# Blocks of 512 tokens in two of three passes over a feed-forward layer, one accumulation carried across the passes, and the next layer taken from the far end

## The chip, the cores and the metric

The kernel runs on one core of one Trainium2 chip. The metric is the device time of one execution in microseconds (us); less is better. TensorE (PE) multiplies, VectorE (DVE) and ScalarE (ACT) work on elements, GpSimd (POOL) and SyncE (SP) mostly issue DMAs. Every instruction queue runs in order.

## The reference

Three layers over 2304 tokens (4 sequences of 576) with 512 channels: retention in 8 heads of 64, a feed-forward layer of 2048 hidden channels, and a gated one of 1536.

```python
scores = scale * np.matmul(q, k.transpose(0, 1, 3, 2))
ret = np.matmul(scores * Dmat[None], v)            # Dmat: decay by head, lower triangle
x = ret.transpose(0, 2, 1, 3).reshape(B * S, H * D)

h = x @ w_in                                       # layer 1: 512 -> 2048 -> 512
g = np.where(h >= 1, h, np.where(h <= -1, 0.0, (h + 1) ** 2 / 4))
x = g @ w_out

out = ((x @ w_a) * (x @ w_b)) @ w_out2             # layer 2: 512 -> 1536 -> 512
```

## The kernel before, in words

All products are made from float32 values split into a high and a low part, so that one product of 128x128 weights is three matmuls (high by high, high by low, low by high). Activations lie with channels in the partitions and tokens in the columns; a matmul takes a block of TB = 384 tokens, and there are NB1 = 6 blocks. All of them pass through `mm` (L156), so every PE row of the profile has line L157; the name of the tile tells the stage.

**Layer 1** is done in three passes over the 16 chunks of 128 hidden channels (GROUPS1, L26): pass 1 takes the first 3, 4 or 6 chunks of a block, pass 2 goes on to chunk 10, pass 3 takes chunks 11 to 15. A step is one chunk f of one block: `l1` (L648) makes `ph` by 12 matmuls from x and w_in; `act1_parts` (L658) runs ACT twice (L661, L662), DVE (L664), and splits the result into the two halves of a tile `g` on ACT (L669) and DVE (L671); `l2` (L688) adds 12 matmuls from g and w_out into the block's four `acc` banks. `l2` of a step is issued after `l1` of the next, so that 24 matmuls (`l2` of the step before, `l1` of the step after) lie between a `ph` and the use of its `g`. Between passes a block's four banks are emptied to DRAM: `y_out` (L709) copies or adds them, `fetch_y` (L704) brings the partial sums back before the next pass' end. The x of each block is written to DRAM in pass 1 (`xd`) and fetched again for each block of pass 2 and 3 (`fetch_x`, L644), at the second step of the block ahead (L1206). Finished blocks go to DRAM as `yf`.

**Layer 2** works in three super-blocks of 768 tokens. `load_y` (L723) reads a super-block into the tile `b`, on POOL's queue. `right` (L743) forms sums of its four quarters with DVE (the first is L757) and splits them on ACT (L739) and DVE (L740) into seven right factors `tx`. A `Quad` (L797) makes one 2x2 block of a product from seven products of 6 matmuls each in banks qx, qy and qz; `keep` (L788, ACT L793) copies a bank to a tile of the pool t2, so that the bank can go on, and DVE combines them (L815, L822, L828). The seventh product goes on in the bank of c22, so PE has to wait for that copy. `act2` (L844) multiplies the two halves of the gate, of which the first (L848) is c11 of both quads, and splits them for the second product (L840, L841).

Pass 1 is in an order written out by hand. From pass 2 on the order of each engine is set by a scheduler that simulates the program; weights are converted in between, from raw tiles that POOL's queue fetches (L184), as credits allow (PACE, L1164).

For super-block 0, `b` is asked for at the start of block 3 of pass 3 (L1198), and the factors are made during block 5, the last. Pools: t2 has 8 buffers of 384 columns (partial sums, kept banks), g has 3, tx and b are opened before pass 2.

Of the kernel before, what the change touches and what calls it, by code (L numbers as in the profile page):

```python
# [36 lines left out]
CHUNKS = 4  # L37
SPARE, INTER_FIRST = (4, 5), 6
# [81 lines left out]
def retention_ffn_kernel(  # L120
# [21 lines left out]
    gpool = ctx.enter_context(tc.tile_pool(name="g", bufs=3))  # L142
# [89 lines left out]
    for f in range(GROUPS1[-1][-1][1]):  # L232
# [3 lines left out]
        for i, blocks in enumerate(GROUPS1) for b, fs in enumerate(blocks) for f in range(*fs)  # L236
# [400 lines left out]
    def x_space(name):  # L637
        return [dpool.tile([P, 2, NCC, TB], F32, name=f"{name}{b}") for b in range(NB)]

    xd = x_space("xd")  # L640
    yd = [[dpool.tile([P, NCC, TB], F32, name=f"y{i}_{b}") for b in range(NB)] for i in range(2)]
    yf = [dpool.tile([P, NCC, TB], F32, name=f"yf{b}") for b in range(NB)]

    def fetch_x(b, space):  # L644
        t = xpool.tile([P, 2, NCC, TB], F32R, tag="x", name="x")
        nc.sync.dma_start(t.bitcast(F32), space[b])
        return t


    def l1(x, w):  # L650
# [8 lines left out]
    def act1_parts(ph):  # L659
        t = tpool.tile([P, TB], F32, tag="t", name="t")  # L660
        nc.scalar.activation(t, ph[:, :TB], AF.Relu, bias=0.5, scale=0.5)  # L661
        nc.scalar.activation(t, t, AF.Square)  # L662
        yield
        nc.vector.scalar_tensor_tensor(  # L664
            out=t, in0=t, scalar=1.0, in1=ph[:, :TB], op0=ALU.min, op1=ALU.max
        )
        yield
        g = gpool.tile([P, 2, TB], F32R, tag="g", name="g")
        hi = nc.scalar.copy(g[:, 0, :], t)  # L669
        yield g  # L670
        anchor[:] = [hi, nc.vector.tensor_sub(g[:, 1, :], t, g[:, 0, :].bitcast(F32))]  # L671
        yield

    def act1(ph, between=lambda: None):
        parts = act1_parts(ph)
# [12 lines left out]
    def l2(step, out=True):  # L688
        i, b, f, first, last = step
        if first:  # L690
            ys[i, b] = accs(NCC)
        y, w, g = ys[i, b], weights["o", f], gs.pop(step)
# [9 lines left out]
    yin = {}  # L702

    def fetch_y(i, b):  # L704
        for m in range(NCC):
            t = yin[b, m] = t2pool.tile([P, TB], F32, tag="t2", name="yin")
            nc.sync.dma_start(t, yd[i - 1][b][:, m, :])

    def y_out(i, b):  # L709
        for m, y in enumerate(ys.pop((i, b))):  # L710
            if i == 0:
                own, tag = (t2pool, "t2") if stage else (y1pool, "yst")
                t = own.tile([P, TB], F32, tag=tag, name="yst")
                (nc.scalar.copy if m % 2 or not stage else nc.vector.tensor_copy)(t, y[:, :TB])
            else:
                t = yin.pop((b, m))
                nc.vector.tensor_add(t, y[:, :TB], t)
            (nc.gpsimd if stage is None else nc.sync).dma_start((yd[i] if i < 2 else yf)[b][:, m, :], t)
# [3 lines left out]
    factors, uses, given = {}, {}, {}  # L722

    def load_y(n):

        if n >= NSB:
            return
        t = given[n] = bpool.tile([P, NCC, 2 * HT], F32, tag="b", name="b")
        t0 = 2 * HT * n
        while t0 < 2 * HT * (n + 1):  # L730
            b, o = divmod(t0, TB)
            m = min(TB - o, 2 * HT * (n + 1) - t0)
            at = t0 - 2 * HT * n
            nc.gpsimd.dma_start(t[:, :, at:at + m], yf[b][:, :, o:o + m])
            t0 += m
# [6 lines left out]
    def right(n):  # L742


        if n >= NSB:
            return
        sub = nc.vector.tensor_sub
        b = given.pop(n)
        b11, b12 = b[:, 0:2, 0:HT], b[:, 0:2, HT:]
        b21, b22 = b[:, 2:4, 0:HT], b[:, 2:4, HT:]  # L750
        t = bpool.tile([P, 2, HT], F32, tag="tt", name="tt")
# [36 lines left out]
    def keep(o, own=False):  # L788

        t = (tpool if own else t2pool).tile(  # L790
            [P, TB], F32, tag="t" if own else "t2", name="keep"
        )[:, :HT]
        kept_by[0] = nc.scalar.copy(t, o[:, :HT])  # L793
        return t
# [43 lines left out]
    def split_g(t):  # L838
        g = gpool.tile([P, 2, TB], F32R, tag="g", name="g2")
        nc.scalar.copy(g[:, 0, :HT], t)  # L840
        nc.vector.tensor_sub(g[:, 1, :HT], t, g[:, 0, :HT].bitcast(F32))  # L841
        return g

    def act2(qa, qb):  # L844
# [7 lines left out]
        for j, (ca, cb) in enumerate(((qa.c12, qb.c12), (qa.c22, qb.c22))):  # L852
            t = late[f + j] = (
                ca if f + 2 == NF2 else ypool[0].tile([P, HT], F32, tag="y", name="gl")
# [77 lines left out]
    def second_layer(n, quad, other):  # L932


        t0, t1 = 2 * HT * n, 2 * HT * n + HT
# [47 lines left out]
    def l2_2(ys, f, g):  # L983
        w = weights[f]
        for m in (0, 2, 3, 1):
            ws = slice(m * P, (m + 1) * P)
            for i, (a, z) in enumerate(((0, 0), (1, 0), (0, 1))):
                mm(
                    ys[m][:, :HT], w[:, a, ws], g[:, z, :HT],
# [39 lines left out]
    def end_tile(keep=0):  # L1029
# [15 lines left out]
    steps = [  # L1045
        (i, b, f, f == f0, f == f1 - 1)
        for i, blocks in enumerate(GROUPS1) for b, (f0, f1) in enumerate(blocks)
        for f in range(f0, f1)
    ]

    def needed(step):
# [20 lines left out]
        "E": lambda b: nc.gpsimd.dma_start(xd[b], xt[b].bitcast(F32)),  # L1072
    }

    def first_product(k):
        i, b, f, *_ = steps[k]
        ph, ops = l1(xt[b], weights["i", f])
        for o in ops:
            mm(*o)
        gen[k] = act1_parts(ph)  # L1080
# [20 lines left out]
    for s, step in enumerate(steps[:last_by_hand]):  # L1101
# [13 lines left out]
        ph, ops = l1(x, weights["i", f])  # L1115
# [8 lines left out]
        gs[step] = act1(ph, between)  # L1124
# [10 lines left out]
        if first:  # L1135
            nc.gpsimd.dma_start(xd[b], x.bitcast(F32))
# [10 lines left out]
    stage = first_sb.enter_context(tc.tile_pool(name="stage", bufs=1))  # L1147

# [5 lines left out]
    for s, step in enumerate(steps):  # L1154
# [4 lines left out]
        if (i, b, first) == (1, NB - 3, True):  # L1159
            raws2.held = True  # L1160
        if (i, b) == (1, NB - 3) and f >= f1 - 3:
            raws1.fetch_to(2 * GROUPS1[1][0][1] + f - f1 + 4)
        if (i, b, first) == (2, NB - 2, True):
            depth[0], raw_every[0], raw_pools[1:] = 2, 5, []  # L1164
        credit += 1.0 if i == 0 else PACE
# [5 lines left out]
        while credit >= 1.0:  # L1171
            with behind():
                make_more(2 * GROUPS1[1][0][1] if i == 0 or (i == 1 and b < NB - 2) else len(stream))
            credit -= 1.0
        if first:
            if i == 0:
                x = xt[b]
            else:
                x = xt.pop((i, b)) if (i, b) in xt else fetch_x(b, xd)
        ph, ops = l1(x, weights["i", f])  # L1180
# [4 lines left out]
        gs[step] = act1(ph)  # L1185
# [3 lines left out]
        if i == 0 and first:  # L1189
            nc.sync.dma_start(xd[b], x.bitcast(F32))  # L1190
        if i > 0 and first:
            fetch_y(i, b)
        if i == 2 and b == 3 and first:
            load_y(0)
        if i == 2 and b == NB - 1 and first:
            making = right(0)
        if i == 2 and b == NB - 1:
            for _ in range(1 + (not first)):  # L1198
                make_right()
        if f == f0 + 1:  # L1200
            ni, nb = (i, b + 1) if b + 1 < NB else (i + 1, 0)
            if 0 < ni < 3:
                xt[ni, nb] = fetch_x(nb, xd)
        if i == 2 and b == NB - 1:
            load_to(9)

    rx.close()
    ypool[0] = first_sb.enter_context(tc.tile_pool(name="y", bufs=NF2 - 2))
# [10 lines left out]
    for n in range(NSB):  # L1219
# [61 lines left out]
        for j, (acc_of, f, _) in enumerate(todo):  # L1281
# [7 lines left out]
            if j == NF2 - 1:  # L1289
                o_out(ys2, 2 * HT * n + HT)  # L1290
        o_out(early, 2 * HT * n)
# [26 lines left out]
```

## Time and profile before

| | |
|---|---|
| median of 3 runs | 875.59 us (874.38 to 876.51) |
| the profiled execution | 874.88 us, of which the span of its instructions is 873.0 us |
| granted clock of TensorE over the span | 0.998 |
| PE busy | 862.5 us (99%) |
| PE weight loads busy (they overlap PE) | 847.7 us (97%) |
| DVE, ACT, POOL busy | 577.4 us (66%), 446.5 us (51%), 81.1 us (9%) |
| DMA | 238.31 MB, mean 273 GB/s |

How to read it: the profile is of one execution. Pass 1 and the retention end at about 190 us of the span, passes 2 and 3 run to 476 us, layer 2 from there to 873 us. The durations of matmuls are those of a pipeline: the next one starts before the last one's time is over, so the price of a matmul is the distance between two starts. "Released by" is the event that ended an idle time.

### The profile page before, as it was taken

The numbers are of one execution on the slowest core, as the hardware profiler recorded it, in microseconds if no ns is written. First come the engines' busy times: TensorE is split into PE (matmuls) and PEld (weight loads), VectorE is DVE, ScalarE is ACT, GpSimd is POOL, SyncE is SP. The second block draws the span as 40 slices with busy tenths as digits, with TensorE's granted clock in tenths as the row PEclk, the third lists the DMA queues.
The fourth block names the chain that finished last, engine by engine and source line by source line (L and its number), as shares of the span: only waits on it lengthen the run. The fifth ranks groups of instructions, "written<-read, shape, count | busy, mean of one in ns | idle before, by whom it ended". The sixth has DMA issues, their size and how long they took to land.

```text
span 873.0 us, 16378 instructions
## 1 busy us (share of the span) xinstructions
PE 862.5 (99%) x6308; PEld 847.7 (97%) x6308; DVE 577.4 (66%) x1088; ACT 446.5 (51%) x899; POOL 81.1 (9%) x124
## 2 busy tenths in 40 slices
PE   8899999999999999999999999999999999999998
PEld 6799999999999999999999999999999999999998
DVE  5787556576777789777779858752347575246465
ACT  4556355575766677666567546442233353333253
POOL 2313233110010011011001000000000000000000
PEclk9999999999999999999999999999999999999999
DMA  9997581648679889899889998879547589847583
GB/s 337 356 337 255 204 279 58 263 149 315 241 258 329 309 291 322 329 352 331 286 302 323 404 410 263 257 245 338 174 145 245 187 276 413 324 146 245 185 288 151
DMA packets 81373, 238.31 MB, mean 273 GB/s; under 512 B 8424, under 2 KB 35304, under 8 KB 78992
## 3 DMA queue, kind: packets, MB, share of 16 engines
q1 hardware_dynamic: 71616, 196.87, 63.2%
q0 software_dynamic: 9664, 40.37, 13.4%
q8 instruction: 50, 0.82, 0.4%
q14 instruction: 27, 0.22, 0.1%
q10 hardware_dynamic: 16, 0.02, 0.0%
HBM read 175.89 MB, written 61.34 MB: 272 GB/s over the span
## 4 chain that ended last, share of the span: by engine, by line
PE 99%; issue 1%; DVE 0%; ACT 0%
PE acc L157 35%; PE ph L157 23%; PE qx L157 17%; PE qy L157 9%; PE late L157 4%; PE qz L157 4%; PE po L157 4%; PE s L157 2%; PE idle L157 1%; PE wacc L157 0%; DVE keep L849 0%; DVE warm L1001 0%; ACT ost L976 0%
## 5 line engine op out<-in xcount | busy, mean ns | idle before, releaser
L157 PE MATMUL acc<-g,w 128*128 128x384 f32 x1296 | 249.0, 334 | 0.0
L157 PEld LDWEIGHTS acc<-g,w 128*128 128x128 f32 x1296 | 226.5, 188 | 0.4
L157 PE MATMUL ph<-x,w 128*128 128x384 f32 x1152 | 220.9, 336 | 0.0
L157 PEld LDWEIGHTS ph<-x,w 128*128 128x128 f32 x1152 | 201.6, 188 | 0.8 <-issue 0.2
L157 PE MATMUL qx<-tx,w 128*128 128x384 f32 x864 | 164.7, 334 | 0.0
L157 PEld LDWEIGHTS qx<-tx,w 128*128 128x128 f32 x864 | 151.1, 188 | 0.0
L793 ACT COPY keep<-qx 128x384 f32<-128x384 f32 x126 | 59.6, 480 | 141.3 <-PE qx L157 133.5
L661 ACT ACTIVATE t<-ph 128x384 f32<-128x384 f32 x96 | 47.1, 490 | 79.3 <-PE ph L157 75.1
L664 DVE SCALAR_TENSOR_TENSOR t<-t,ph 128x384 f32<-128x384 f32 x96 | 52.8, 551 | 51.9 <-ACT t L662 51.5
L157 PE MATMUL qy<-tx,w 128*128 128x384 f32 x432 | 86.3, 334 | 0.0
L157 PE MATMUL acc<-sp,w 128*128 128x384 f32 x432 | 77.5, 334 | 0.0
L157 PEld LDWEIGHTS qy<-tx,w 128*128 128x128 f32 x432 | 75.9, 188 | 0.0
L157 PEld LDWEIGHTS acc<-sp,w 128*128 128x128 f32 x432 | 75.1, 188 | 0.0
L669 ACT CAST g<-t 128x384 fp32r<-128x384 f32 x96 | 49.0, 510 | 40.7 <-DVE t L664 34.8
L671 DVE TENSOR_TENSOR g<-t,g 128x384 fp32r<-128x384 f32 x96 | 53.5, 557 | 20.8 <-ACT g L669 20.5
L886 DVE TENSOR_TENSOR sp<-gb,sp 128x768 fp32r<-128x768 f32 x42 | 40.1, 956 | 21.3 <-ACT sp L885 21.0
L662 ACT ACTIVATE t<-t 128x384 f32<-128x384 f32 x96 | 50.5, 526 | 2.7
L885 ACT CAST sp<-gb 128x768 fp32r<-128x768 f32 x42 | 35.1, 837 | 32.3 <-PE acc L157 18.8
L196 ACT ACTIVATE raw<-raw 128x512 int32<-128x512 uint32 x68 | 45.6, 671 | 2.7 <-DMA raw<-in_moe_w_out 2.7
L828 DVE TENSOR_TENSOR keep<-keep 128x384 f32<-128x384 f32 x36 | 20.0, 557 | 40.4 <-ACT keep L793 40.4
L157 PE MATMUL qz<-tx,w 128*128 128x384 f32 x216 | 43.4, 334 | 0.0
L815 DVE TENSOR_TENSOR keep<-qz,keep 128x384 f32<-128x384 f32 x36 | 20.0, 556 | 32.1 <-PE qz L157 27.7
(113 smaller groups left out, 944.9 us busy)
## 6 DMA issues: line engine op xcount, KB each, us to landing
w<-q SPq DMA_DIRECT2D x126, 512.0 KB, 5.3
q<-q SPq DMA_DIRECT2D x42, 512.0 KB, 7.1
w<-o SPq DMA_DIRECT2D x42, 512.0 KB, 5.1
x<-xd SPq DMA_DIRECT2D x12, 1536.0 KB, 8.6
u<-in_qkv SPq DMA_DIRECT2D x32, 512.0 KB, 8.3
raw<-in_moe_w_out POOLq DMA_DIRECT2D x18, 512.0 KB, 6.5
yin<-y SPq DMA_DIRECT2D x48, 192.0 KB, 4.3
xd<-x POOLq DMA_DIRECT2D x5, 1536.0 KB, 8.7
```

Of the source, the lines that this page charges most:

```text
L157: return nc.tensor.matmul(o, l, r, start=start, stop=stop, skip_group_check=goes_on)
L196: nc.scalar.activation(r, low, AF.Copy, scale=2.0 ** -29)
L661: nc.scalar.activation(t, ph[:, :TB], AF.Relu, bias=0.5, scale=0.5)
L662: nc.scalar.activation(t, t, AF.Square)
L664: nc.vector.scalar_tensor_tensor(out=t, in0=t, scalar=1.0, in1=ph[:, :TB], op0=ALU.min, op1=ALU.max)
L669: hi = nc.scalar.copy(g[:, 0, :], t)
L671: anchor[:] = [hi, nc.vector.tensor_sub(g[:, 1, :], t, g[:, 0, :].bitcast(F32))]
L793: kept_by[0] = nc.scalar.copy(t, o[:, :HT])
L815: anchor[:] = [kept_by[0], nc.vector.tensor_add(self.c11, z[:, :HT], self.c11)]
L828: nc.vector.tensor_add(self.c22, self.c22, self.s5)
L885: nc.scalar.copy(t[:, 0], b)
L886: nc.vector.tensor_sub(t[:, 1], b, t[:, 0].bitcast(F32))
```

## The change

From token 768 on, passes 2 and 3 work in blocks of 512 tokens: blocks 0 and 1 of 384, then three of 512 (NWIDE = 5). Pass 1 keeps its six blocks, so x and the partial sums of tokens 768 to 2303 lie in one DRAM tile each, whose slices both sizes address. The blocks of pass 3 come in the order 4, 3, 2, 0, 1. Block 4, the last of pass 2, is the first of pass 3 and goes on in its four banks: it isn't emptied and fetched in between. The x tiles of blocks 4 and 3 stay in two pools (xw0, xw1) from pass 2 to pass 3. Super-blocks run from the last tokens to the first. The tiles t, g become 512 wide, g's halves are tiles of their own; t2 has 7 buffers in place of 8, and `gl` of the first chunk takes a buffer of the conversion pool. The pools of the factors are opened on the other side of memory, before the last two blocks of pass 3, where `b` is now asked for too (second-last block).

```diff
+WIDE = 512
+NWIDE = 2 + 3 * (NB1 - 2) // 4
 GROUPS1 = [
     [(0, 3), (0, 4)] + [(0, 6)] * (NB1 - 2),
-    [(3, 11), (4, 11)] + [(6, 11)] * (NB1 - 2),
-    [(11, 16)] * NB1,
+    [(3, 11), (4, 11)] + [(6, 11)] * (NWIDE - 2),
+    [(11, 16)] * NWIDE,
 ]
+PASSES = [range(NB1), range(NWIDE), [4, 3, 2, 0, 1]]
...
-    gpool = ctx.enter_context(tc.tile_pool(name="g", bufs=3))
+    gpool = ctx.enter_context(tc.tile_pool(name="g", bufs=6))
...
+    def width(i, b):
+        return WIDE if i and b > 1 else TB
...
+    xd = in_parts("xd", (2, NCC))
+    y0 = in_parts("y0", (NCC,))
...
-                ops.append((ph[:, :TB], w[:, a, ws], x[:, z, cc, :]))
+                ops.append((ph[:, :n], w[:, a, ws], x[:, z, cc, :]))
...
-                mm(y[m][:, :TB], w[:, a, ws], g[:, z, :], first and n == 0, last and n == 2)
+                mm(y[m][:, :k], w[:, a, ws], g[z], first and n == 0, last and n == 2)
...
+    def first_token(n):
+        return 2 * HT * (NSB - 1 - n)
...
+                ca if f + 2 == NF2
+                else ypool[0].tile([P, HT], F32, tag="y", name="gl") if f
+                else cpool.tile([P, 512], F32, tag="conv", name="gl")[:, :HT]
...
+                (i, b, f, f == f0 and (i, b) != (2, goes_on), f == f1 - 1 and (i, b) != (1, goes_on))
...
-    t2pool = ctx.enter_context(tc.tile_pool(name="t2", bufs=8))
-    txpool = ctx.enter_context(tc.tile_pool(name="tx", bufs=5))
-    bpool = ctx.enter_context(tc.tile_pool(name="b", bufs=1))
+    t2pool = ctx.enter_context(tc.tile_pool(name="t2", bufs=7))
...
+    wide[:] = [
+        ground.enter_context(tc.tile_pool(name=f"xw{n}", bufs=1, side="right")) for n in range(2)
+    ]
+    ywide[0] = ground.enter_context(tc.tile_pool(name="yw", bufs=YBUFS, side="right"))
...
+        if (i, b, begins) == (2, PASSES[2][-2], True):
+            ground.close()
+            rx.close()
+            txpool[0] = ctx.enter_context(tc.tile_pool(name="tx", bufs=5, side="right"))
+            bpool[0] = ctx.enter_context(tc.tile_pool(name="b", bufs=1, side="right"))
-        credit += 1.0 if i == 0 else PACE
+        credit += 1.0 if i == 0 else PACE * width(i, b) / TB
...
-        if i == 2 and b == 3 and first:
+        if i == 2 and b == PASSES[2][-2] and begins:
             load_y(0)
...
-            if 0 < ni < 3:
-                xt[ni, nb] = fetch_x(nb, xd)
+            if (ni, nb) in ((2, goes_on), (2, goes_on - 1)):
+                xt[ni, nb] = xt[1, nb]
+            else:
+                xt[ni, nb] = fetch_x(ni, nb)
...
-    ypool[0] = first_sb.enter_context(tc.tile_pool(name="y", bufs=NF2 - 2))
+    ypool[0] = first_sb.enter_context(tc.tile_pool(name="y", bufs=NF2 - 4))
```

How the scheduler's order moves, at the three places that the prediction speaks of. In brackets stand the semaphores that an instruction waits for: DMAHW and DMASW are DMAs, the others engines; PE, without waits, shows its order alone.

**SP, at the end of pass 1.** First before, where the spill of the last x, the fetch of x for block 0 of pass 2 and the first partial sums follow each other:

```order
L1190 DMA xd5_180<-x_2153 128x3072 [waits DMAHW5_49,DVE_49]
L646 DMA x_2606<-xd0_175 128x3072 [waits DMASW5_49,DMASW2_49,DMAHW6_49,DMASW0_49,PE_49]
L718 DMA y0_4_185<-yst_2544 128x384 [waits DMAHW7_49,Activation_49]
L718 DMA y0_4_185<-yst_2541 128x384 [waits DMAHW0_49,DVE_49]
L718 DMA y0_4_185<-yst_2550 128x384 [waits DMAHW1_49,Activation_49]
L718 DMA y0_4_185<-yst_2547 128x384 [waits DMAHW2_49,DVE_49]
L646 DMA x_2882<-xd1_176 128x3072 [waits DMAHW3_49,DMASW7_49,DMAHW5_49,DMASW1_49,PE_49]
```

and now, where the xw are 512 wide and xdw and y0w are the DRAM tiles of tokens from 768 on:

```order
L740 DMA yin_3546<-y0w_180 128x512 [waits DMASW6_49,DMASW4_49]
L1248 DMA xdw_177<-x_2164 1024x1x384 [waits DVE_49]
L672 DMA xw_3602<-xdw_177 128x8x512 [waits DMAHW2_49,DMASW7_49,DMASW5_49]
L672 DMA x_2628<-xd0_175 128x3072 [waits DMAHW3_49,PE_49]
L672 DMA xw_3269<-xdw_177 128x8x512 [waits DMAHW4_49,DVE_49]
L753 DMA y0w_180<-yst_2565 128x384 [waits DMAHW5_49,Activation_49]
L753 DMA y0w_180<-yst_2562 128x384 [waits DMAHW6_49,DVE_49]
L753 DMA y0w_180<-yst_2571 128x384 [waits DMAHW7_49,Activation_49]
L753 DMA y0w_180<-yst_2568 128x384 [waits DMAHW0_49,DVE_49]
```

The fetch of x for block 0 now stands behind four partial sums of block 2 and the first wide x (2048 KB), and another wide x stands behind it.

**ACT and DVE, at the start of super-block 0.** ACT before; keep_5919 and keep_5835 are c11 of the two quads, keep_5927 is c22 of the first:

```order
L793 COPY keep_5919<-qx_5912 128x384 [waits DMAHW6_49,DMAHW5_49,PE_49]
L220 CAST w_5728<-stage_5722 128x512 [waits DVE_49]
L793 COPY keep_5880<-qx_5828 128x384 [waits PE_49]
L196 ACTIVATE raw_5779<-raw_5779 128x512 [waits DMASW7_49,Activation_49]
L220 CAST w_5776<-stage_5722 128x512 [waits DVE_49]
L382 CAST qo_5896<-stage_5722 128x256 [waits DVE_49]
L793 COPY keep_5927<-qx_5828 128x384 [waits DMAHW7_49,PE_49]
```

ACT now; keep_5537 and keep_5621 are c11 of the two quads, keep_5629 is c22 of the first:

```order
L832 COPY keep_5663<-qx_5614 128x384 [waits PE_49]
L386 CAST qo_5598<-stage_5423 128x256 [waits DVE_49]
L386 CAST qo_5672<-stage_5423 128x256 [waits DMAHW1_49,DMAHW4_49,DVE_49,PE_49]
L386 CAST qo_5672<-stage_5423 128x256
L832 COPY keep_5629<-qx_5530 128x384 [waits DVE_49]
L880 CAST g2_5739<-keep_5537 128x384
```

DVE now, where keep_5621 is completed, read for the last time, and then c22 is worked on:

```order
L380 TENSOR_TENSOR stage_5423<-stage_5423 128x256 [waits DVE_49]
L387 TENSOR_TENSOR qo_5598<-stage_5423,qo_5598 128x256 [waits Activation_49]
L854 TENSOR_TENSOR keep_5621<-qz_5641,keep_5621 128x384 [waits DMAHW2_49,PE_49]
L888 TENSOR_TENSOR keep_5537<-keep_5621,keep_5537 128x384 [waits DVE_49]
L387 TENSOR_TENSOR qo_5672<-stage_5423,qo_5672 128x256 [waits DMAHW4_49,DMAHW1_49,Activation_49]
L387 TENSOR_TENSOR qo_5672<-stage_5423,qo_5672 128x256 [waits Activation_49]
L867 TENSOR_TENSOR keep_5629<-keep_5629,keep_5546 128x384 [waits Activation_49]
```

PE now, around it; tx_5516 goes on in the bank that keep_5629 copies:

```order
L161 MATMUL qx_5530<-tx_5470,w2_5307 128x384 x6
L161 MATMUL qx_5614<-tx_5470,w2_5417 128x384 x6
L161 MATMUL qz_5641<-tx_5411,w2_5365 128x384 x6
L161 MATMUL qx_5696<-tx2_5299,w2_5419 128x384 x6
L161 MATMUL qx_5530<-tx_5516,w2_5309 128x384 x6
L161 MATMUL acc0_5522<-g2_5739,w_4820 128x384 x2
```

The copy of c22 waited for PE and a DMA before and waits for DVE now: its tile of pool t2 is that of keep_5621, which L888 (L848 before) reads last.

**POOL, in the last blocks of pass 3.** Before, the first piece of `b` (384 tokens) is asked for two raw tiles ahead of the second:

```order
L184 DMA raw_4919<-in_moe2_w_a 128x4x128 [waits DMASW7_49,DVE_49,Activation_49]
L734 DMA b_5146<-yf0_193 128x4x384 [waits DMAHW4_49,DMAHW2_49,DMAHW5_49,DMAHW1_49,DMAHW6_49,DMAHW0_49,PE_49]
L184 DMA raw_4964<-in_moe2_w_a 128x4x128 [waits DMASW2_49,DVE_49]
L184 DMA raw_5096<-in_moe2_w_b 128x4x128 [waits DMASW1_49,DVE_49,Activation_49]
L734 DMA b_5146<-yf1_194 128x4x384 [waits DMAHW2_49,DMAHW7_49,DMAHW1_49,DMAHW0_49]
L184 DMA raw_5157<-in_moe2_w_b 128x4x128 [waits DMASW3_49,DVE_49,Activation_49]
```

and now:

```order
L188 DMA raw_5006<-in_moe2_w_b 128x4x128 [waits DMASW1_49,DVE_49,Activation_49]
L188 DMA raw_5013<-in_moe2_w_b 128x4x128 [waits DMASW4_49,DVE_49,Activation_49]
L188 DMA raw_5203<-in_moe2_w_out 128x512 [waits DMASW6_49,DVE_49,Activation_49]
L772 DMA b_5064<-yf3_189 128x4x256 [waits DMAHW3_49,DMAHW4_49,DMAHW2_49,DMAHW5_49,DMAHW1_49,DMAHW6_49,DMAHW0_49,DMAHW7_49,DMASW3_49,DVE_49]
L772 DMA b_5064<-yf4_190 128x4x512
L188 DMA raw_5243<-in_moe2_w_out 128x512 [waits DMASW5_49,DMASW0_49,DVE_49]
```

Both pieces (256 and 512 tokens) are asked for together, behind three raw tiles that wait for ACT and DVE.

## Rows read from the trace of the kernel before

**Rows 1.** The page: busy time, and the chain that ended last.

```profile
PE 862.5 (99%) x6308; PEld 847.7 (97%) x6308; DVE 577.4 (66%) x1088; ACT 446.5 (51%) x899; POOL 81.1 (9%) x124
...
PE 99%; issue 1%; DVE 0%; ACT 0%
```

**Rows 2.** Windows: PE, PEld, DVE, ACT, POOL busy us; clock, DMA share, GB/s.

```profile
190.00:362.00 172.00, 172.00 (x994) 172.00 (x994) 134.66 (x281) 114.56 (x243) 19.56 (x28) 1.00 0.82 288
362.00:476.00 114.00, 114.00 (x660) 114.00 (x659) 90.40 (x189) 72.72 (x157) 8.89 (x13) 1.00 0.90 321
```

**Rows 3.** The chain, one of its pieces: start, us, what, number of instructions.

```profile
702.76 23.23 PE acc L157 x134
```

**Rows 4.** PE's timeline, 512-wide matmuls: start, us, what.

```profile
12.60 0.50 PE L157 MATMUL idle<-warm 128*128 128x512 f32 x1
...
12.93 0.39 PE L157 MATMUL idle<-warm 128*128 128x512 f32 x1
...
13.16 0.40 PE L157 MATMUL idle<-warm 128*128 128x512 f32 x1
```

**Rows 5.** PE's timeline, 384-wide matmuls behind a wait.

```profile
582.72 0.44 PE L157 MATMUL late<-g,w 128*128 128x384 f32 x1 [0.65 <-DVE keep L849]
...
583.00 0.34 PE L157 MATMUL late<-g,w 128*128 128x384 f32 x1
...
583.17 0.34 PE L157 MATMUL late<-g,w 128*128 128x384 f32 x1
```

**Rows 6.** Groups by form, 190 to 476 us: busy, mean ns, idle before.

```profile
L157 PE MATMUL acc<-g,w 128*128 128x384 f32 x814 | 156.8, 334 | 0.0
...
L664 DVE SCALAR_TENSOR_TENSOR t<-t,ph 128x384 f32<-128x384 f32 x67 | 36.8, 551 | 29.7 <-ACT t L662 29.3
...
L205 DVE SCALAR_TENSOR_TENSOR stage<-raw,stage 128x512 uint32<-128x512 uint32 x27 | 18.6, 689 | 0.5
```

**Rows 7.** Timeline at the start of super-block 0, PE, DVE and ACT.

```profile
478.41 1.20 PE L157 MATMUL qz<-tx,w 128*128 128x384 f32 x6
...
480.46 0.55 DVE L815 TENSOR_TENSOR keep<-qz,keep 128x384 f32<-128x384 f32 x1
481.05 0.56 DVE L848 TENSOR_TENSOR keep<-keep 128x384 f32<-128x384 f32 x1
...
481.70 0.48 ACT L793 COPY keep<-qx 128x384 f32<-128x384 f32 x1 [0.70 <-DVE keep L848]
```

**Rows 8.** Timeline at 581 us: PE, then DVE released by it.

```profile
580.86 1.20 PE L157 MATMUL qx<-tx,w 128*128 128x384 f32 x6
...
582.10 0.56 DVE L849 TENSOR_TENSOR keep<-qx,keep 128x384 f32<-128x384 f32 x1 [0.25 <-PE qx L157]
```

**Rows 9.** POOL's timeline, the last spill of x on it, and PE then.

```profile
151.49 0.54 POOL L1136 DMA_DIRECT2D xd<-x  x1
...
152.01 0.09 POOL L559 MEMSET turn<- 1x1 f32 x1
...
152.65 0.46 PE L157 MATMUL po<-ret,u 64*64 64x64 f32 x16
```

**Rows 10.** Fetch of x for pass 2: issue, first use, landing.

```profile
169.73 0.33 SPq L646 DMA_DIRECT2D x<-xd  x1
...
194.50 0.68 PE L157 MATMUL ph<-x,w 128*128 128x384 f32 x3
...
x<-xd SPq DMA_DIRECT2D x12, 1536.0 KB, 8.6
```

**Rows 11.** Fetch of b: last block's start, first use, POOL's wait, landing.

```profile
446.17 0.51 PE L157 MATMUL ph<-x,w 128*128 128x384 f32 x2
...
453.23 0.95 DVE L757 TENSOR_TENSOR tt<-b 128x768 f32<-128x768 f32 x1
...
471.17 0.53 POOL L184 DMA_DIRECT2D raw<-in_moe_w_out  x1 [27.51 <-ACT keep L793]
...
b<-yf POOLq DMA_DIRECT2D x6, 768.0 KB, 9.0
```

More of the change, by code (lines that the diff above doesn't have):

```diff
@@ L37 @@
 CHUNKS = 4
+YBUFS = 5
 SPARE, INTER_FIRST = (4, 5), 6
@@ L235, in retention_ffn_kernel @@
         f: (i, b)
-        for i, blocks in enumerate(GROUPS1) for b, fs in enumerate(blocks) for f in range(*fs)
+        for i, blocks in enumerate(GROUPS1) for b in PASSES[i] for f in range(*blocks[b])
     }
@@ L634, in rounds_to, with first_of, in_parts, part @@
             output_next()
[L637 to L646, printed above, removed]
+    def width(i, b):
+        return WIDE if i and b > 1 else TB
+    def first_of(b):
+        return TB * b if b < 2 else 2 * TB + WIDE * (b - 2)
+    def in_parts(name, shape):
+        two = [dpool.tile([P, *shape, TB], F32, name=f"{name}{b}") for b in range(2)]
+        rest = dpool.tile([P, *shape, NB * TB - 2 * TB], F32, name=f"{name}w")
+        def part(i, b):
+            n = width(i, b)
+            return two[b] if b < 2 else rest[(slice(None),) * (1 + len(shape)) + (
+                slice(n * (b - 2), n * (b - 1)),)]
+        return part
+    xd = in_parts("xd", (2, NCC))
+    y0 = in_parts("y0", (NCC,))
+    y1, yf = (
+        [dpool.tile([P, NCC, width(1, b)], F32, name=f"{name}{b}") for b in range(NWIDE)]
+        for name in ("y1", "yf")
+    )
+    wide, ywide, ground = [None, None], [None], ExitStack()
+    def fetch_x(i, b):
+        if b < 2:
+            t = xpool.tile([P, 2, NCC, TB], F32R, tag="x", name="x")
+        else:
+            t = wide[b % 2].tile([P, 2, NCC, WIDE], F32R, tag="xw", name="xw")
+        nc.sync.dma_start(t.bitcast(F32), xd(i, b))
         return t
-    def l1(x, w):
+    def l1(x, w, n):
         ph = bank("ph")
@@ L664, in act1_parts, with act1 @@
         nc.vector.scalar_tensor_tensor(
-            out=t, in0=t, scalar=1.0, in1=ph[:, :TB], op0=ALU.min, op1=ALU.max
+            out=t, in0=t, scalar=1.0, in1=ph[:, :n], op0=ALU.min, op1=ALU.max
         )
         yield
[L668 to L671, printed above, removed]
+        high = gpool.tile([P, WIDE], F32R, tag="g", name="g")[:, :n]
+        hi = nc.scalar.copy(high, t)
+        low = gpool.tile([P, WIDE], F32R, tag="g", name="g")[:, :n]
+        yield high, low
+        anchor[:] = [hi, nc.vector.tensor_sub(low, t, high.bitcast(F32))]
         yield
-    def act1(ph, between=lambda: None):
-        parts = act1_parts(ph)
+    def act1(ph, n, between=lambda: None):
+        parts = act1_parts(ph, n)
         next(parts)
@@ L689, in l2 @@
         i, b, f, first, last = step
+        k = width(i, b)
         if first:
-            ys[i, b] = accs(NCC)
-        y, w, g = ys[i, b], weights["o", f], gs.pop(step)
+            ys[b] = accs(NCC)
+        y, w, g = ys[b], weights["o", f], gs.pop(step)
         for m in range(NCC):
@@ L702, in retention_ffn_kernel, with partial @@
     yin = {}
+    def partial(i, b):
+        return y0(i, b) if i < 1 or i == 1 or b == NWIDE - 1 else y1[b]
     def fetch_y(i, b):
         for m in range(NCC):
-            t = yin[b, m] = t2pool.tile([P, TB], F32, tag="t2", name="yin")
-            nc.sync.dma_start(t, yd[i - 1][b][:, m, :])
+            own, tag, n = (ywide[0], "yw", WIDE) if b > 1 else (t2pool, "t2", TB)
+            t = yin[b, m] = own.tile([P, n], F32, tag=tag, name="yin")
+            nc.sync.dma_start(t, partial(i, b)[:, m, :])
     def y_out(i, b):
-        for m, y in enumerate(ys.pop((i, b))):
+        n = width(i, b)
+        to = y0(i, b) if i == 0 else (y1 if i == 1 else yf)[b]
+        for m, y in enumerate(ys.pop(b)):
             if i == 0:
@@ L727, in load_y @@
             return
[L728 to L735, printed above, removed]
+        t = given[n] = bpool[0].tile([P, NCC, 2 * HT], F32, tag="b", name="b")
+        t0 = first_token(n)
+        for b in range(NWIDE):
+            lo, hi = max(t0, first_of(b)), min(t0 + 2 * HT, first_of(b) + width(1, b))
+            if lo < hi:
+                nc.gpsimd.dma_start(
+                    t[:, :, lo - t0:hi - t0], yf[b][:, :, lo - first_of(b):hi - first_of(b)]
+                )
     def split_right(n, j, o):
@@ L838, in split_g @@
     def split_g(t):
[L839 to L842, printed above, removed]
+        high = gpool.tile([P, WIDE], F32R, tag="g", name="g2")[:, :HT]
+        low = gpool.tile([P, WIDE], F32R, tag="g", name="g2")[:, :HT]
+        nc.scalar.copy(high, t)
+        nc.vector.tensor_sub(low, t, high.bitcast(F32))
+        return high, low
     def act2(qa, qb):
@@ L1044, in retention_ffn_kernel @@
     prev = None
[L1045 to L1049, printed above, removed]
+    steps, goes_on = [], NWIDE - 1
+    for i, spans in enumerate(GROUPS1):
+        for b in PASSES[i]:
+            f0, f1 = spans[b]
+            steps += [
+                (i, b, f, f == f0 and (i, b) != (2, goes_on), f == f1 - 1 and (i, b) != (1, goes_on))
+                for f in range(f0, f1)
+            ]
+    after = {}
+    for a, z in zip(steps, steps[1:]):
+        if a[:2] != z[:2]:
+            after[a[:2]] = z[:2]
     def needed(step):
@@ L1122, in between @@
                 begin_tile()
-        gs[step] = act1(ph, between)
+        gs[step] = act1(ph, TB, between)
         end_tile(1)
@@ L1172, in retention_ffn_kernel @@
             with behind():
-                make_more(2 * GROUPS1[1][0][1] if i == 0 or (i == 1 and b < NB - 2) else len(stream))
+                make_more(2 * GROUPS1[1][0][1] if i == 0 or (i == 1 and b < NWIDE - 2) else len(stream))
             credit -= 1.0
-        if first:
+        if begins:
             if i == 0:
@@ L1184, in retention_ffn_kernel @@
             used(("i", f))
-        gs[step] = act1(ph)
+        gs[step] = act1(ph, width(i, b))
         if prev:
@@ L1189, in retention_ffn_kernel @@
         if i == 0 and first:
-            nc.sync.dma_start(xd[b], x.bitcast(F32))
-        if i > 0 and first:
+            nc.sync.dma_start(xd(0, b), x.bitcast(F32))
+        if i > 0 and begins and (i, b) != (1, goes_on):
             fetch_y(i, b)
-        if i == 2 and b == 3 and first:
+        at_end = i == 2 and b == PASSES[2][-1]
+        if i == 2 and b == PASSES[2][-2] and begins:
             load_y(0)
-        if i == 2 and b == NB - 1 and first:
+        if at_end and begins:
             making = right(0)
-        if i == 2 and b == NB - 1:
-            for _ in range(1 + (not first)):
+        if at_end:
+            for _ in range(1 + (not begins)):
                 make_right()
-        if f == f0 + 1:
-            ni, nb = (i, b + 1) if b + 1 < NB else (i + 1, 0)
-            if 0 < ni < 3:
-                xt[ni, nb] = fetch_x(nb, xd)
-        if i == 2 and b == NB - 1:
+        if f == f0 + 1 and (i, b) in after:
+            ni, nb = after[i, b]
+            if (ni, nb) in ((2, goes_on), (2, goes_on - 1)):
+                xt[ni, nb] = xt[1, nb]
+            else:
+                xt[ni, nb] = fetch_x(ni, nb)
+        if at_end:
             load_to(9)
-    rx.close()
-    ypool[0] = first_sb.enter_context(tc.tile_pool(name="y", bufs=NF2 - 2))
+    ypool[0] = first_sb.enter_context(tc.tile_pool(name="y", bufs=NF2 - 4))
     quad, waiting, pending = None, [], [lambda: l2(prev)]
```

51 lines of the change are left out of this document (27 added, 24 removed).

## The prediction

> **What bounds the kernel now.** I read the page first: PE is busy 862.5 us and the chain that ended last is 99% PE [rows 1]. The windows come next: in passes 2 and 3, which this change cuts anew, PE has no gap at all (172.00 of 172 us, then 114.00 of 114) at a granted clock of 1.00, while DVE stands at 134.66 of 172 us and ACT at 114.56 [rows 2]. So in that stretch only two things count: how long PE's own instructions take, and whether something new makes PE wait. Other engines' savings are worth nothing by themselves. No idle time stands before the 814 matmuls from g in this stretch [rows 6].
>
> **The matmuls: -2.0 us.** Blocks 2 to 5 of 384 tokens have 4 x (5 + 5) = 40 steps of 24 matmuls in passes 2 and 3, 960 in all; three blocks of 512 have 3 x 10 = 30 steps, 720. The columns are the same (368,640), so only a fixed share of each matmul can be saved. The old price is exact: 134 matmuls in a row take 23.23 us [rows 3], 0.1734 us each, and 960 take 166.4 us. At 384 columns that is 13 ns over the 160 ns that the columns take at 2.4 GHz, the higher level of the clock, which is the granted one here.
>
> The new price has few rows. Three matmuls of 512 columns stand near the start of the program: 12.60, 12.93, 13.16 [rows 4], two distances in 0.56 us. The first follows a wait, and the first distance after a wait is longer, so I set them against three of 384 columns that follow a wait too: 582.72, 583.00, 583.17 [rows 5], 0.45 us. The difference is 0.11 us for two times 128 columns, 55 ns for 128. So a matmul of 512 costs 0.1734 + 0.055 = 0.2284 us, 720 of them 164.4 us: 2.0 less. Bounds: if only the columns are added (128 at 2.4 GHz, 53.3 ns), 0.2267 us and -3.2; if the price goes with the width, 0.2311 us and 0.0. I take the middle one, because it is what the rows of that shape show; the second distance alone (0.23 against 0.17) says the same.
>
> Against these rows stands a rule. The Trainium skill, "TensorE: Matmul & The Clock Gate", section "Back-to-back issue gap", gives N/2.4 + 2.5 ns for one isolated matmul at the higher clock, that is 215.8 ns for 512. By it 720 matmuls would take 155.4 us, 11.0 less than the rows' 166.4. The trace disagrees with it at 384 columns (162.5 ns by the rule, 173.4 measured) and in the 0.23 us above.
>
> **The other engines in the wide steps: 0.** A `g` is made by five operations on ACT and DVE, covered by 24 matmuls. DVE takes 551 ns for 384 columns and 689 ns for 512 [rows 6], a factor of 1.25; the cover grows by 0.2284/0.1734 = 1.32. So the cover grows at least as fast as what it hides, and DVE's and ACT's shares of the stretch can only fall. Block 4's partial sums, no longer stored, fetched and added, save DVE four additions and SP eight DMAs, beside a busy PE: 0. If the cover were gone, a wide step would show idle time before `acc`, at most some tenths of a us in each of 30 steps.
>
> **The copy of c22 at the start of super-block 0: +0.9 us.** With t2 one buffer smaller, c22 of the first quad takes the tile of the other quad's c11. The order shows that ACT's copy now waits for DVE, PE's second product after qz goes on in that bank, and in between stand one product of six matmuls. The chain from the start of qz's six matmuls: 1.20 us until they end [rows 7], 0.04 until DVE starts (582.06 to 582.10) [rows 8], 0.55 for the addition, 0.04, 0.56 for the product that reads the tile last, 0.09 until ACT starts (481.61 to 481.70), 0.48 for the copy [rows 7], and 0.06 until PE starts (582.66 to 582.72) [rows 5, 8]: 3.02 us. PE has 12 matmuls until then, 2.08 us. The stall is 0.94 us. Queued behind the copy on ACT is the split of g2, which PE uses six matmuls later; it moves along and costs nothing more. Bounds: 0 below, if DVE's semaphore stands for an earlier instruction than L888; 1.8 above, since in the profile DVE came to that addition at 480.46, 0.85 us after qz's end (479.61) [rows 7], busy with its queue, which nobody waited for then. A gain is excluded: PE doesn't wait there now. I take 0.9, as four partial sums of 384 columns are added ahead of it before as after.
>
> **The spill of x on POOL: +0.1 us.** `xd` of blocks 2 to 4 is now written in 1024 rows of one DRAM tile in place of 128. Issuing 128 rows took POOL 0.54 us at 151.49; the flag that it sets next (152.01, 0.09 us) lies 0.55 us ahead of the matmuls that follow it [rows 9]. No row has 1024 rows. Bounds: 0, and 0.5 if the issue takes as long again and the 0.55 us are no slack; I take 0.1, nearer to 0, because the flag has that lead.
>
> **The fetch of x for pass 2: 0.** SP issues it at 169.73, and PE needs it at 194.50; such a fetch of 1536 KB lands in 8.6 us [rows 10]. Now it stands behind a wide x of 2048 KB, four partial sums (256 KB each) and a spill. SP doesn't wait for that spill, since the wide x put ahead covers other tokens. At the 288 GB/s of this stretch [rows 2], the spill, the wide x, the fetch and the other wide x (7.3 MB) take 25 us; x is third of these, so some 18 us after 165.4. Cover: PE's work up to 194.50. If it is gone, PE stands until x lands.
>
> **The fetch of b: 0.** DVE first uses b 7.06 us into the last block (446.17 to 453.23) [rows 11]. It is now asked for in the block before, which lasts 5 x 24 x 0.1734 = 20.8 us, so 27.9 us later at the latest. It stands behind three raw tiles on POOL, and lands in 9.0 us [rows 11]. Up to 17 us on POOL's queue are covered (27.9 less 9.0 and two issues); I expect some 5, as the order has the tiles freed early in the block.
>
> **Sum.** -2.0 + 0.9 + 0.1 = -1.0 us. On the profiled execution, 874.88 us (span 873.0 and 1.9 around it), that is 873.9; this execution lies 0.7 under the median, so the median becomes 875.59 - 1.0 = 874.6 us. A difference of 0.2% (1.75 us) is about what a measurement of this kernel can tell from no change, so this counts as no change.
>
> **The rivals.**
> *Only the columns are paid, or the copy is hidden (faster).* -3.2 with the copy's 0.9 and POOL's 0.1 is 873.4; -2.0 to -3.2 with no stall is 873.6 to 872.4. For it: at 384 columns 13 ns lie over the columns' time, which looks like a fixed part. Against it: 55 ns rather than 53.3 in rows 4 and 5, and the plain wait for DVE.
> *Weight loads pace the 384-wide matmuls (much faster).* PE's weight loader is busy through the whole stretch too (172.00 of 172) [rows 2]; if it sets the 173 ns, 512 columns cost their 213.3 ns alone, 153.6 us, -12.8 and 863.8 with the other terms. Against it: 0.23 us in rows 4. By the rule of the Trainium skill above, with the same terms, it would be 865.6.
> *b comes late (slower).* POOL waited 27.5 us for ACT at a raw tile at 471.17 [rows 11], and b now stands behind three such tiles. If the last of them waits that long, b is issued 10.5 us later than the 17 that are covered. DVE waits at its first sum of b, in order, with the `g` of the following steps queued behind it, so after the 24 matmuls of cover (4.2 us) PE stands for the remaining 6.3: 880.9. It decides from a wait of 17 us on. Against it: the other raw tiles behind DVE and ACT in this stretch are freed with each converted chunk.
> *x comes late (slower).* In series, at 8.6 us for 1536 KB, spill, wide x and fetch would take 28.7 us, to 194.1, and half of the other wide x another 5.7: 5.3 us late, 879.9. Against it: the 288 GB/s above.
> *The change doesn't do what it says:* no; the order shows 240 matmuls fewer.
>
> **How the numbers follow.** My sum, with terms that stay within 1.75 us of the median: 0.44. Faster by more: 0.38, of which 0.33 for the columns or the hidden copy, and 0.05 for the weight loads. Slower by more: 0.18, of which 0.07 for b, 0.05 for x, and 0.06 for a copy at its upper bound with matmuls that go with the width (0.0 + 1.8 + 0.5 = +2.3, 877.9). The range goes from 871.9, the lowest of the first rival less half a us for the runs' scatter, to that 877.9; outside are 0.05 below and most of b and x above.
>
> **What would show it.** The chain should show 720 matmuls of 512 columns in distances of 0.228 us (0.227 or 0.231 decide between the bounds), PE without idle time in passes 2 and 3, and an idle time of some 0.9 us before a qx group near the start of super-block 0, released by ACT's copy. Wrong would be: distances of 0.216 or less (then it is the weight loads), idle time before the first `ph` of pass 2 (x), or idle time in the last block of pass 3 behind DVE (b).

## The result, and the profile after

The changed kernel takes 881.05 us (median of 6 runs, 880.33 to 882.8) against 875.47 for the kernel before (6 runs): ratio 1.007, 95% interval 1.0057 to 1.0083. It is slower by 5.6 us, outside the range of 871.9 to 877.9. The profiled execution took 882.8 us, the highest of the six; 1.2 us of its excess over the profiled execution of the kernel before lie in the first 35 us, where inputs arrive.

The page of the changed kernel, busy time and chain:

```profile
PE 870.1 (99%) x6068; PEld 821.8 (93%) x6068; DVE 574.3 (65%) x1056; ACT 443.2 (50%) x869; POOL 81.8 (9%) x124
...
PE 99%; issue 1%; DVE 0%; ACT 0%; DVEq 0%
```

PE executes 240 matmuls fewer and is busy 7.6 us longer than in [rows 1]. So most of the time did not go into waiting; the matmuls themselves became slower. To see it in rows, I count the matmuls that fit into a window in which PE never idles: 280 to 400 us, where the changed kernel runs wide steps only, and 620 to 700 us, where super-blocks run. The kernel before (columns as in [rows 2]):

```profile
280.00:400.00 120.00, 120.00 (x694) 120.00 (x693) 99.92 (x211) 82.49 (x177) 15.62 (x22) 1.00 0.90 318
620.00:700.00 80.00, 80.00 (x463) 80.00 (x462) 45.66 (x75) 30.59 (x59) 0.00 (x0) 1.00 0.56 183
```

The changed kernel:

```profile
280.00:400.00 120.00, 120.00 (x518) 97.14 (x518) 91.18 (x173) 78.12 (x149) 13.04 (x19) 1.00 0.70 244
620.00:700.00 80.00, 80.00 (x457) 80.00 (x456) 40.85 (x68) 27.78 (x55) 0.00 (x0) 1.00 0.52 172
```

In the second window the matmuls have 384 columns in both kernels, at a granted clock of 1.00 in both, and 463 have become 457: 1.3% slower, in a stage whose products the change doesn't touch. In the first, 120 us hold 518 wide matmuls (one or two reach over the edges), some 232 ns each. Three pieces of the chain and a row of the timeline, all of the changed kernel, narrow it down:

```profile
320.60 2.76 PE acc L161 x12
323.36 4.21 PE ph L161 x18
...
709.02 23.23 PE acc L161 x134
```

```profile
651.22 2.28 PE L161 MATMUL qx<-tx,w 128*128 128x384 f32 x12
```

and a row of the timeline of the kernel before, for as many factor products:

```profile
479.45 2.24 PE L157 MATMUL qx<-tx,w 128*128 128x384 f32 x12
```

A wide `ph` costs 4.21/18 = 234 ns, a wide `acc` 2.76/12 = 230. The 134 matmuls from `sp` still take 23.23 us, as in [rows 3], but 12 factor products take 2.28 us from the first start to the last end, where they took 2.24. Not every matmul is slower; those that read the factors `tx` and the wide x are, and some that run among them. Over the whole trace, starts lie 176.55 ns apart on average for the 1080 products that read tx, 174.6 for the 432 that read tx2 (they stand between the others), 234.1 for wide `ph` and 230.0 for wide `acc`, which reads g.

What tx and the wide x share is the side of on-chip memory: the change opened their pools on the right. The built programs say where tiles start (byte in the partition, modulo 512):

```
tile           before   changed
weights w      128      128
x, g, sp, tx2  128      128
tx             128      480
wide x (xw)    -        480
```

From here on, a tile's distance in bytes is its start less the start of the weights that are used with it, modulo 256 (the runs below show why 256); tx and xw now lie at a distance of 96 (480 less 128 is 352). tx2 and the g of the wide `acc` lie at 0, as before, and are slower all the same. The trace shows when: the first five wide `acc` behind a `ph` take 231.4 ns on average, the tenth to twelfth in a row 226.9; products from tx2 take 175.1 among the first six behind products from tx, and 173.5 from the seventh on. So a matmul can be slow because of those before it, up to some nine back.

### The profile page after: what moved, and what is told of

It reads as the page before. It is cut to its first block, busy times and chain, and to the rows that moved or that the text cites. A ratio compares the mean times of both kernels' runs of the same rounds, so it can differ in the third digit from the quotient of the medians.

```text
span 881.0 us, 15795 instructions
## 1 busy us (share of the span) xinstructions
PE 870.1 (99%) x6068; PEld 821.8 (93%) x6068; DVE 574.3 (65%) x1056; ACT 443.2 (50%) x869; POOL 81.8 (9%) x124
## 4 chain that ended last, share of the span: by engine, by line
PE 99%; issue 1%; DVE 0%; ACT 0%; DVEq 0%
PE acc L161 34%; PE ph L161 23%; PE qx L161 17%; PE qy L161 9%; PE qz L161 4%; PE late L161 4%; PE po L161 4%; PE s L161 2%; PE idle L161 1%; PE wacc L161 0%; DVE keep L854 0%; DVE g L698 0%; DVE keep L889 0%; DVE warm L1044 0%; ACT ost L1019 0%
## 5 line engine op out<-in xcount | busy, mean ns | idle before, releaser
L161 PE MATMUL acc<-g,w 128*128 128x384 f32 (+1 forms) x1176 | 246.4, 353 | 0.2 <-DVE g L698 0.2
L161 PE MATMUL ph<-x,w 128*128 128x384 f32 x672 | 127.8, 337 | 0.0
L161 PEld LDWEIGHTS ph<-x,w 128*128 128x128 f32 x672 | 117.3, 188 | 1.1 <-DVE t L690 0.2
L161 PE MATMUL ph<-xw,w 128*128 128x512 f32 x360 | 91.6, 396 | 0.0
L690 DVE SCALAR_TENSOR_TENSOR t<-t,ph 128x384 f32<-128x384 f32 (+1 forms) x86 | 51.3, 598 | 53.0 <-ACT t L688 52.8
L687 ACT ACTIVATE t<-ph 128x384 f32<-128x384 f32 (+1 forms) x86 | 45.4, 527 | 76.0 <-PE ph L161 72.3
L161 PEld LDWEIGHTS ph<-xw,w 128*128 128x128 f32 x360 | 67.6, 188 | 16.0
L698 DVE TENSOR_TENSOR g<-t,g 128x384 fp32r<-128x384 f32 (+1 forms) x86 | 51.6, 601 | 23.9 <-ACT g L695 20.5
L695 ACT CAST g<-t 128x384 fp32r<-128x384 f32 (+1 forms) x86 | 47.2, 549 | 37.8 <-DVE t L690 34.8
L688 ACT ACTIVATE t<-t 128x384 f32<-128x384 f32 (+1 forms) x86 | 48.4, 563 | 2.3
```

What stands on the lines that cost most here:

```text
L161: return nc.tensor.matmul(o, l, r, start=start, stop=stop, skip_group_check=goes_on)
L687: nc.scalar.activation(t, ph[:, :n], AF.Relu, bias=0.5, scale=0.5)
L690: nc.vector.scalar_tensor_tensor(out=t, in0=t, scalar=1.0, in1=ph[:, :n], op0=ALU.min, op1=ALU.max)
L695: hi = nc.scalar.copy(high, t)
L698: anchor[:] = [hi, nc.vector.tensor_sub(low, t, high.bitcast(F32))]
```

## The experiments

**Is it the address or the place? (e1_edge32)** An unused tile of 32 bytes first on the right side of the changed kernel; every instruction stays in its order.

```diff
+    edge = ctx.enter_context(tc.tile_pool(name="edge", bufs=1, side="right"))
+    edge.tile([P, 8], F32, tag="edge", name="edge")
     rx = ExitStack()
```

> The changed kernel with one unused tile of 32 bytes opened first on the right side of on-chip memory, so that every tile of that side moves down by 32 bytes and starts on a multiple of 64; the order of the instructions stays. Theory A (address): a matmul whose moving tile starts at 32 modulo 64 is slower; then the distance of factor products goes from 176.5 back to 173.3 ns, that of the wide products from 234 (xw) and 230 (g) to 226.7 ns, and the time from 881.05 to 881.05 - 1512 x 2.7 ns - 360 x 7.4 ns - 360 x 3.3 ns - 0.4 = 872.7 us. Theory B (place): the right side itself, where DMAs write beside these tiles, is slow; then 881 us and the same distances. Theory C (the width and the reversed order themselves): 881 us too.

Measured: 876.63 us, ratio 1.002 (1.0007 to 1.0033) to the kernel before, 874.69 in these runs. Moving the tiles by 32 bytes gave back over half of the loss, so neither theory B nor theory C can be the whole of it. But A's number was missed: tx products came to a mean of 173.2 ns with a wide scatter (169 to 176), their neighbours from tx2 became slower (175.3), and wide ones cost 230. The scatter of the tx products lies in the first six of each run of them (173.0 on average); from the seventh on they take 173 to 174, as at a distance of 0. A multiple of 64 is not enough for the wide ones. Theory A also counted the 230 ns of g to its address, though g starts at 128.

**The kernel before, with its factors moved by 32 and by 64 bytes (e2_tx32, e3_tx64).**

```diff
+    lead = ctx.enter_context(tc.tile_pool(name="lead", bufs=1))
+    lead.tile([P, 8], F32, tag="lead", name="lead")
     txpool = ctx.enter_context(tc.tile_pool(name="tx", bufs=5))
+    trail = ctx.enter_context(tc.tile_pool(name="trail", bufs=1))
+    trail.tile([P, 24], F32, tag="trail", name="trail")
```

(16 and 16 in place of 8 and 24 for 64 bytes.)

> The kernel before with its factor pool (tx, left side) moved up by 32 bytes, to 32 modulo 64; 96 bytes behind it keep all later pools on a multiple of 64. Theory A (address): the factor products read from tx go from 173.3 to some 176.5 ns, those from tx2 to some 174.6, as in the changed kernel, and the time rises by 1080 x 3.2 + 432 x 1.3 ns = 4.0 us to 879.5. Theories B and C: no change, 875.5.

> The kernel before with its factor pool moved up by 64 bytes (from 0 to 64 modulo 128), later pools as in the run above. Theory A with 64 bytes as the unit: no change, 875.5. Theory A with 128 bytes as the unit: 879.5 as in the run above.

Measured: 876.99 (1.0025, 1.0009 to 1.0041) and 877.19 (1.0037, 1.0019 to 1.0054). Both are slower, neither by the amount expected. The single stages said why. With 32 bytes, tx products cost only 174.0 ns; but in the two runs those that read `sp` cost 175.9 and 175.6, and those that read tx2 174.4 and 175.2. The 128 bytes of the two extra pools had moved `sp` too, from 128 to 0 modulo 256, which I had taken for harmless. So `sp`, now 128 bytes away from the weights modulo 256, is slow, and a multiple of 128 isn't enough either.

**The weights moved by 32 bytes (e4_w32)**, everything behind them by 128 (the two pools as above, around the pool w).

> The kernel before with its weight pool moved up by 32 bytes, to 32 modulo 64, everything behind it on a multiple of 64. If the address matters for what is loaded as weights too, and the loader (97% busy) passes it on, up to 5000 matmuls x 3.2 ns = 16 us more, 891; if it matters only for the moving operand, 875.5.

Measured: 888.57 (1.0152, 1.0133 to 1.0172), 13.9 us slower. All products whose weights lie in that pool take 176.7 ns, whatever they read. Those whose weights lie in the pool wx, at 0 modulo 256 like their moving tiles, take 173.4. The distance between the two starts would explain both (0 less 160 is 96 modulo 256, and 96 is also the distance of tx and xw from the weights in the changed kernel, with the same 176.6); that the weights' own place does it is still open here.

**The changed kernel at distance 0 (theory D, e5_same512).** 352 bytes ahead of the wide x and of tx:

```diff
+    edge = ground.enter_context(tc.tile_pool(name="edge", bufs=1, side="right"))
+    edge.tile([P, 88], F32, tag="edge", name="edge")
     wide[:] = [
...
+            edge = ctx.enter_context(tc.tile_pool(name="edge2", bufs=1, side="right"))
+            edge.tile([P, 88], F32, tag="edge", name="edge")
             txpool[0] = ctx.enter_context(tc.tile_pool(name="tx", bufs=5, side="right"))
```

> The changed kernel with an unused tile of 352 bytes ahead of the wide x tiles and another ahead of the factors, so that xw and tx start at 128 modulo 512, where the weights and all moving tiles of the kernel before start too. Theory D: what counts is the distance of the moving tile's start from the weights' start, modulo some unit of 256 or 512 bytes; at distance 0 every matmul takes its shortest time. Then all distances of 384 are 173.3 ns again, those of 512 are 226.7 ns (wide steps 3.2 us cheaper than before), the stall at c22 (0.8) and the 0.5 us lost near 97 us stay: 1.9 us under the kernel before. Theory A (multiples of 64 bytes are enough): as in run e1_edge32, 2 us above the kernel before.

Measured: 873.08 (12 runs), ratio 0.9971 (0.9956 to 0.9987) to 874.73: 1.65 us faster than the kernel before, where 1.9 was expected. Its windows:

```profile
280.00:400.00 120.00, 120.00 (x531) 99.38 (x530) 94.11 (x182) 78.79 (x152) 13.05 (x19) 1.00 0.71 248
620.00:700.00 80.00, 80.00 (x463) 80.00 (x462) 46.51 (x76) 30.95 (x60) 0.00 (x0) 1.00 0.54 183
```

and the piece of its chain that answers to the one above:

```profile
321.34 4.08 PE ph L161 x18
```

463 again, and a wide matmul costs 4.08/18 = 226.7 ns. The wide `acc`, whose own tiles and weights did not move, come down from 230.0 to 226.9 with the `ph` between them. Nothing but addresses differs from the changed kernel, and tx and xw still lie on the right side: theories B and C fall. Some of this settling is left even here: where wide matmuls follow on those of 384 columns, the first nine take 224 to 236 ns (231 on average), all at distance 0, and the next ones 226 to 227. Between the two, each against the kernel before in its own runs, lie 5.58 + 1.65 = 7.2 us.

**Where the unit ends, and whether the common place matters (e8_tx256, e9_all32).** The factors of the kernel before 256 bytes further up (64 and 64 in the two pools); then its whole left side 32 bytes further up, weights included (the lead pool ahead of w, no trail).

> The kernel before with its factor pool 256 bytes further up (384 in place of 128 modulo 512), later pools 512 bytes further up. Theory D with a unit of 256 bytes: no change, all distances 173.3 ns. With a unit of 512 bytes: factor products slower by 2 to 3 ns, some 3 us more.

> The kernel before with everything on the left side, weights and moving tiles alike, 32 bytes further up (160 in place of 128 modulo 256). If only the distance between the moving tile's start and the weights' start counts (theory D): all distances stay 173.3 ns, and the time does not change. If the place of the weights itself counts (the rival that run e4_w32, where they lay at 160 too, leaves open): every product some 3.3 ns slower, 14 us more.

Measured: 875.3 (1.0002, 0.9985 to 1.0019) and 874.81 (0.9994, 0.9985 to 1.0004): no change that can be told, factor products and those from `sp` at 173.3 to 173.5 ns from start to start in both. So 256 bytes further is no distance, while 128 bytes (`sp` above) was one: the unit is 256 bytes. The place itself costs nothing, so it is the distance that counts. In the window of super-blocks, weights alone at 160 and all at 160:

```profile
620.00:700.00 80.00, 80.00 (x456) 80.00 (x455) 39.35 (x66) 25.80 (x52) 0.00 (x0) 1.00 0.51 177
```

```profile
620.00:700.00 80.00, 80.00 (x463) 80.00 (x462) 45.42 (x74) 30.45 (x59) 0.00 (x0) 1.00 0.56 183
```

**The wait at the start of super-block 0 (e6_same512_c22).** In the changed kernel's timeline it reads

```profile
482.17 1.23 PE L161 MATMUL qz<-tx,w 128*128 128x384 f32 x6
483.43 0.56 DVE L854 TENSOR_TENSOR keep<-qz,keep 128x384 f32<-128x384 f32 x1 [0.87 <-PE qz L161]
484.02 0.56 DVE L888 TENSOR_TENSOR keep<-keep 128x384 f32<-128x384 f32 x1
484.04 2.43 PE L161 MATMUL qx<-tx,w 128*128 128x384 f32 x12 [0.65 <-DVE keep L854]
484.61 0.48 ACT L832 COPY keep<-qx 128x384 f32<-128x384 f32 x1 [1.60 <-DVE keep L888]
```

PE loses 0.82 us (0.99 from the last qz start to the next, less 0.17) and some 0.16 more in two longer steps behind it (0.28 and 0.23 us between starts), but one product earlier than forecast, released by DVE's L854 and not by ACT's copy: qx_5696, which the scheduler set ahead of c22's product, takes the very bank (4) that L854 has just emptied of qz. When that is done, ACT's copy is through (485.09) before the seventh matmul of the row starts (485.19). The edit gives the first quad's c22 a tile of another pool:

```diff
-            self.c22 = keep(self.x)
+            if self.at == (0, 0, 0):
+                self.c22 = ypool[0].tile([P, HT], F32, tag="y", name="keep")
+                nc.scalar.copy(self.c22, self.x[:, :HT])
+            else:
+                self.c22 = keep(self.x)
```

> The run above, and the first quad's c22 is copied to a tile of the pool that gl uses later, in place of a t2 tile. If the stall of 0.8 us near 483 us comes from the tile that c22 shares with the other quad's c11, it is gone, and the time is 0.8 us under the run above. Rival: PE waits there for DVE's other work or for ACT, and the stall stays or another takes its place.

Measured: 872.52 (0.9968, 0.9955 to 0.9982), 0.56 under the run before it, with intervals that overlap: the time alone doesn't show the gain. The trace shows that the wait is gone. With a free tile the order of PE, ACT, DVE and SP moved, and the scheduler now puts c22's product directly behind qz, so PE runs on:

```profile
477.17 1.20 PE L161 MATMUL qz<-tx,w 128*128 128x384 f32 x6
...
478.21 1.20 PE L161 MATMUL qx<-tx,w 128*128 128x384 f32 x6
```

In this profile another wait, of 0.3 us, ends at 753.0.

**The halves of g (e7_same512_c22_pair).** In the changed kernel PE waits once in pass 1, near 97 us, and loses 0.5 us; DVE stood before a low half of g for 3.29 us until PE had read an older one:

```profile
96.28 0.56 DVE L698 TENSOR_TENSOR g<-t,g 128x384 fp32r<-128x384 f32 x1 [3.29 <-PE acc L161]
...
96.89 2.02 PE L161 MATMUL acc<-g,w 128*128 128x384 f32 x10 [0.20 <-DVE g L698]
```

```diff
-        high = gpool.tile([P, WIDE], F32R, tag="g", name="g")[:, :n]
+        g = gpool.tile([P, 2, WIDE], F32R, tag="g", name="g")
+        high, low = g[:, 0, :n], g[:, 1, :n]
         hi = nc.scalar.copy(high, t)
-        low = gpool.tile([P, WIDE], F32R, tag="g", name="g")[:, :n]
```

(and so for g2, with 3 tiles in place of 6.)

> The run above, with the halves of g in one tile again (three tiles of two halves of 512 in place of six halves; the same memory). If the 0.5 us that PE waits for DVE's g at 97 us, in the stage written out by hand, come from the separate halves, they are gone, and the time is 0.5 us under the run above (some 3 us under the kernel before). Rival: they come from the timing of the inputs at the start, and nothing changes.

Measured: 873.38 (0.9978, 0.9962 to 0.9994), not under the run before it. The wait itself is gone from the trace, as expected, but a new one of 0.3 us ends at 487.9, and waits for inputs at the start differ by as much. Inconclusive for the time.

## Why the prediction was wrong, point by point

- **What bounds the kernel** held: PE alone, at 99%, at a granted clock of 0.998.
- **The step that failed** is one that the sum didn't have: "only two things count: how long PE's own instructions take" was applied to the wide matmuls alone. The pools of the factors and of the wide x were moved to the right side, and I let the 1512 factor products keep their 173.3 ns without a word: a term at nothing without a reason. They took 176.55 (tx) and 174.6 (tx2): 1080 x 3.2 + 432 x 1.3 ns = 4.0 us came from there. The rows of before couldn't show it, since there all weights and tiles of these matmuls start at the same byte modulo 256. The pools' new addresses could have been read from the built program; that they matter could not.
- **The matmuls, -2.0:** measured +0.7 (360 x 234.1 + 360 x 230.0 ns = 167.1 us against 166.4), by the same addresses. At distance 0 the price is 226.9 to 227.0 ns, and 720 cost 163.4 us: -3.0, next to the lower bound ("only the columns are added"). The three rows of `idle` that I weighed it by were 1.5 ns too dear; PE has no idle time before the first of them, while the three of 384 columns that they were set against stand behind one of 0.65 us [rows 5]. The rival of the weight loads falls: the loader idles in the wide steps (99.38 busy of 120), and the matmul still costs some 13.5 ns over the time of its columns, as it did at 384. The Trainium skill, "TensorE: Matmul & The Clock Gate", section "Back-to-back issue gap", has a formula for one isolated matmul that makes 215.8 ns of 512 columns. The wide matmuls here took 226.9 on average at the best distance, so this stream doesn't reach it.
- **c22, +0.9:** the size was right (0.82, or 1.0 with the two longer steps behind it), the way was not, so the size was luck: the order moved with the smaller pool, and PE waited for a bank that DVE had to empty, one product before the bank that I looked at. The prediction's chain had read each bank's name, not which names share a bank.
- **POOL, +0.1:** no PE wait there. 1024 rows took 0.90 us in place of 0.54.

```profile
153.22 0.90 POOL L1186 DMA_DIRECT2D xdw<-x  x1
```

- **The fetches of x and b, 0 each:** right. PE has no idle time before pass 2's first `ph` nor in the last block of pass 3. Both slower rivals, x and b, failed; the time came out on their side by another mechanism.
- **Not foreseen:** the 0.5 us at 97 us, from halves of g that now come free each by itself, in a stage where the order is fixed by hand.

The pieces add up. In the changed kernel, 4.0 for the factor products, 0.7 for the wide ones, 1.0 at c22 and 0.5 at 97 us make +6.2, where 5.6 was measured. With the addresses mended, -3.0 + 1.0 + 0.5 = -1.5, and the run at distance 0 lies 1.65 under the kernel before. The addresses cost 4.0 us on factor products, 3.7 on wide ones (167.1 less 163.4), and some tenths on others; by the medians it is 7.2. The intervals of the two medians, each about 1 us either way or more, cover these differences.

## What to carry to other kernels

When a change moves pools, read where the tiles that the matmuls read end up, and compare it with where the weights start: keep both at the same byte modulo 256, for all matmuls of a stage, since a few at another distance slow those behind them too. If a stage that the change doesn't touch gets slower with PE busy throughout, count matmuls in equal windows before looking for waits. A term that the sum lacks is more dangerous than one that is mis-sized: list what is moved, not only what is added.

## What the runs showed of the hardware

A matmul in a dense stream of 384 columns (float32 in split halves, weights loaded for each) took 173.3 ns when the start of its moving tile and of its weights were equal modulo 256 bytes, 176.0 ns at a distance of 128 and 176.7 at 96. At 32 it took 173.9. At 64 it took 173.3 to 173.4 from the seventh in a row on; the first six scattered (169 to 177 in all but a few), and products at distance 0 that stand among them were slower (tx2 at 175.2 and 175.3). The equal place itself didn't matter (128 and 160 alike). With 512 columns it was 226.9 at distance 0, 230.4 at 64 and 234.1 at 96; wide matmuls at distance 0 that alternate with those took 229.7 and 230.0. In the trace the weight load of a matmul starts some 0.17 us before it, while the one before reads its tile. That these two reads get into each other's way would fit, but no run here separates it from other causes, and why a stream takes some nine matmuls to settle after a change of distance or of width is open too.
